# Up-projections with high and low activations in one stream of 512 columns, and their two halves added on the way out

## The chip, the cores and the metric

The kernel runs on one core of a Trainium2 chip. The metric is the device time of one launch in microseconds, the median of several runs. The core has a matrix engine (TensorE, PE in the profile; its weight loads are listed as PEld), a vector engine (VectorE, DVE), a scalar engine (ScalarE, ACT), GpSimd (POOL) and SyncE (SP), which mostly issues DMAs. In the trace each engine runs its instructions in program order, and engines wait for each other through semaphores.

## What is computed

The reference is banded attention (each row sees itself and the 63 rows before it), then a dense two-layer network with ELU, then a mixture of eight experts in which each token goes to one.

```python
x = attention(q, k, v)                       # 4 batches x 576 rows, 8 heads of 64 -> (2304, 512)
h = x @ w_in                                 # (2304, 2048)
g = np.where(h > 0, h, np.exp(np.minimum(h, 0)) - 1)
x = g @ w_out                                # (2304, 512)
logits = x @ w_gate + modality_bias[modality_id]
e_idx = argmax(logits); gate_w = softmax(logits)[e_idx]
for e in range(8):
    out[e_idx == e] = gate_w * (np.maximum(x[e_idx == e] @ w1[e], 0) @ w2[e])
```

## The kernel before

Every product of the two networks is made of three: an operand `a` is split into a high part and a low part (`hi` and `a - hi`), and the kernel adds high x high, high x low and low x high. The dense network runs over nine groups of 256 tokens and eight pieces of 256 hidden columns, 72 pairs of an up piece and a down piece. The experts run over slots: eight slots of 256 tokens with four up and four down pieces each, and a ninth, wide slot of 384 tokens.

An **up piece** (`h_pass`, called by `f1p` for the dense network and by `e1p` for the slots) makes 256 hidden columns for 256 tokens. For each half `c` of 128 hidden columns and each of the four blocks `d` of the model dimension it issues three matmuls of 256 columns: high weights on high x (L526), high weights on low x (L527), low weights on high x (L528). That is 24 matmuls into one PSUM bank of the pool `ps_h`, which has two. Each matmul has its own weight load. A **down piece** (`y_pass`, L535 to L537) is 12 matmuls of 512 columns into two banks `y`.

Between an up piece and its down piece of the dense network stand, in this order: `f1x` (the negative part of `h`, on ACT at L556 or on DVE at L558), `f1e` (exponential, ACT, L562), `f1m` (DVE, L571, from `e` and `h`), `f1h` (high part into `g`, ACT, L575) and `f1l` (low part, on POOL at L582 or on DVE at L580). The bank `h` is free again after `f1m`, except for the pieces listed in `VIA`, which keep their values in the bank up to `f1l`. In a slot it is shorter: `e1a` (Relu into the high part, ACT, L947), then `e1d` (low part, DVE, L952), and then the down piece `e2p`.

The order of the work on each engine isn't written by hand. `program` lists pieces with an engine, a cost, what they depend on, a rank and the buffers they take and free; `plan` goes through them in planned time, and on each engine starts the ready piece of lowest rank whose buffers are free. The code is then issued in that order. The buffer `L` is no memory: it keeps certain DVE and POOL pieces apart in the plan, but not on the chip. Everything but `sw` is known when the plan is made.

`switch` (piece `sw`) stands three times in each slot from slot 2 on. It reads a register that says whether the next slot has another expert, and only then splits new weights: for each of its tiles 128x1024 a copy on ACT (`e_hi`, L864) and a subtraction on DVE (`e_lo`, L868), two tiles in its first and last place, four in the middle one. Its cost in the plan is 0.3 us whether or not it is taken. With these inputs it is taken once, from slot 4 to slot 5.

The routing of the whole batch (`route_d` and `route2_d`, L759 to L841, small vectors on one partition) runs on DVE as two pieces, `rd` and `r2`.

Of the kernel before, what the change touches and what calls it, by code (L numbers as in the profile page):

```python
# [81 lines left out]
def fused(ctx, tc, q, k, v, w_in, w_out, mod, w_gate, mbias, w1, w2, out):  # L82
# [60 lines left out]
    gp = mkpool("g", 3)  # L143
# [289 lines left out]
    def x_at(t, qds):  # L433
        return (a[:, 2 * qds[0]:2 * qds[-1] + 2, 128 * (t % 2):128 * (t % 2) + 128] for a in X[t // 2])
# [13 lines left out]
    def new_x(g):  # L448
        X[g] = tuple(xp.tile([128, 4, 256], F32R, tag=n, name=n) for n in ("xh", "xl"))
# [62 lines left out]
    G, H, EL = {}, {}, {}  # L512
# [3 lines left out]
    def on_act(g):  # L516
        return g in FXA
# [241 lines left out]
    def route_d():  # L759
# [35 lines left out]
        RT["no"], RT["base"] = no, base  # L795

    def route2_d():
# [103 lines left out]
    def xpa(s, t):  # L901
# [124 lines left out]
    def program():  # L1026
# [79 lines left out]
        for g in range(NG):  # L1106
            for s in range(NP):
# [5 lines left out]
                add(("f1",) + k, "PE", 2.89, f1p, *k, rank=r + 1.5,  # L1113
                    deps=[("wd", "i", s, 0), ("wd", "i", s, 1)] + [("4d", 4 * g + x) for x in ((1, 3) if 2 * g >= T0 else range(4))] + ([("f1", g, s - 1)] if s else [("f1", g - 1 - (g < NG - 1), NP - 1)] if g > 1 else []),
                    need={"h": 1}, free=({"X": 1} if s == NP - 1 else {}) | ({"w": 2} if g == NG - 1 else {}), lat=0.22)
                add(("fx",) + k, "ACT" if on_act(g) else "DVE", 0.48 if on_act(g) else 0.6, f1x, *k, rank=r - 900, deps=[("f1",) + k], need={"e": 1})
# [39 lines left out]
        add("iota", "POOL", 0.6, iotas, rank=-700.0, deps=[("g3s", EC - 4)], need={"w": 1}, lat=0.5)  # L1156
        add("ep", "PE", 0.1, early_p, rank=-2000.0, deps=[("g3d", EC - 1)], need={"ps": 1}, lat=0.22)
# [109 lines left out]
```

## Time and profile before

| | |
|---|---|
| median of 3 runs | 738.29 us (738.16 to 739.16) |
| profiled execution, its own time | 738.16 us |
| its span, first to last instruction | 736.4 us |
| PE busy | 722.5 us, 98% |
| DVE busy | 429.7 us, 58% |
| ACT busy | 326.1 us, 44% |
| POOL busy | 192.7 us, 26% |
| mean granted TensorE clock | 0.998 |

The profiled execution is one launch; 1.8 us of its time lie outside the span. A busy engine has instructions under way, which tells nothing of how close they lie: the profile gives each matmul a modelled end and the ends overlap the next start, so for PE the distance from one start to the next is the number to read.

### The profile page before, as it was taken

The page shows a single profiled execution, that of the slowest core. Times are in us where ns is not written, and L with a number is a line of the kernel's source. Part 1 is how long each engine was busy: PE and PEld are TensorE (multiplying, and loading weights), DVE is VectorE, ACT ScalarE, POOL GpSimd, SP SyncE. Part 2 cuts the span into 40 slices and gives each one's busy share as a digit, 9 for nine tenths or more (in the row PEclk, how much of TensorE's full clock was granted, in tenths as well). Part 3 has the DMA queues.
Part 4 walks back from the last instruction along what each step waited for, and adds up shares of the span by engine and source line. Part 5 has one row for each costly group of instructions (what it writes and reads, how often), then busy time and mean ns, then how long its engine had stood idle before and what let it go on. Part 6 is the DMA issues. An engine that isn't in the chain of part 4 may idle for free. (4 is left out here: it accounts for less than half of the span.)

```text
span 736.4 us, 14731 instructions
## 1 busy us (share of the span) xinstructions
PE 722.5 (98%) x5550; PEld 649.7 (88%) x5550; DVE 429.7 (58%) x1324; ACT 326.1 (44%) x774; POOL 192.7 (26%) x184
## 2 busy tenths in 40 slices
PE   8899999999999999999999999999999999999996
PEld 7788988999899998989898998989988999999995
DVE  5999998688595194296394293793872124321211
ACT  5998753656565364454454433454111114311211
POOL 5211002334334233224233323431031212111011
PEclk9999999999999999999999999999999999999999
DMA  7999811632321131140210000550028112000001
GB/s 197 225 259 319 271 64 53 198 99 59 73 72 30 26 96 24 30 109 8 59 45 1 12 18 6 194 140 20 15 69 305 58 30 75 17 30 30 1 28 46
DMA packets 103102, 62.81 MB, mean 85 GB/s; under 512 B 85777, under 2 KB 90019, under 8 KB 102891
## 3 DMA queue, kind: packets, MB, share of 16 engines
q1 hardware_dynamic: 99403, 52.03, 26.1%
q0 software_dynamic: 3616, 9.72, 4.0%
q8 instruction: 46, 0.75, 0.4%
q14 instruction: 37, 0.30, 0.1%
HBM read 51.05 MB, written 10.94 MB: 84 GB/s over the span
## 5 line engine op out<-in xcount | busy, mean ns | idle before, releaser
L526 PE MATMUL h<-xh,whi 128*128 128x256 f32 x576 | 165.6, 287 | 0.4 <-DVE g L580 0.4
L528 PE MATMUL h<-xh,wlo 128*128 128x256 f32 x576 | 162.9, 283 | 0.0
L527 PE MATMUL h<-xl,whi 128*128 128x256 f32 x576 | 162.9, 283 | 0.0
L582 POOL TENSOR_TENSOR g<-e,g 128x512 fp32r<-128x512 f32 x57 | 80.0, 1403 | 190.8 <-ACT g L575 167.1
L535 PE MATMUL y<-whi,g 128*128 128x512 f32 x288 | 116.0, 403 | 0.0
L536 PE MATMUL y<-wlo,g 128*128 128x512 f32 x288 | 112.7, 391 | 0.0
L537 PE MATMUL y<-whi,g 128*128 128x512 f32 x288 | 112.5, 391 | 0.0
L526 PEld LDWEIGHTS h<-xh,whi 128*128 128x128 f32 x576 | 110.1, 191 | 2.4 <-PE h L528 0.6
L527 PEld LDWEIGHTS h<-xl,whi 128*128 128x128 f32 x576 | 110.3, 191 | 1.3
L528 PEld LDWEIGHTS h<-xh,wlo 128*128 128x128 f32 x576 | 110.2, 191 | 0.1
L571 DVE SCALAR_TENSOR_TENSOR e<-e,h 128x512 f32<-128x512 f32 x57 | 39.1, 686 | 85.6 <-ACT e L562 72.0
L612 DVE CUSTOM_DVE_ANT_0 lgs<-ysb,wgb 128x512 bf16<-128x512 f32 x96 | 79.5, 828 | 2.5 <-ACT ysb L599 0.6
L556 ACT ACTIVATE e<-h 128x512 f32<-128x512 f32 x64 | 38.1, 595 | 94.0 <-PE h L528 93.6
L952 DVE SCALAR_TENSOR_TENSOR g<-h,g 128x512 fp32r<-128x512 f32 x32 | 22.1, 690 | 86.6 <-ACT g L947 86.5
L526 PE MATMUL h<-xh,ehi 128*128 128x256 f32 x256 | 72.6, 284 | 0.0
L528 PE MATMUL h<-xh,elo 128*128 128x256 f32 x256 | 72.4, 283 | 0.0
L527 PE MATMUL h<-xl,ehi 128*128 128x256 f32 x256 | 72.4, 283 | 0.0
L947 ACT ACTIVATE g<-h 128x512 fp32r<-128x512 f32 x32 | 19.1, 597 | 112.8 <-PE h L528 104.2
L537 PEld LDWEIGHTS y<-whi,g 128*128 128x128 f32 x288 | 54.1, 188 | 12.1
L535 PEld LDWEIGHTS y<-whi,g 128*128 128x128 f32 x288 | 54.2, 188 | 10.8 <-issue 1.5
L390 ACT ACTIVATE sm<-sm,st 128x128 f32<-128x128 f32 x144 | 56.0, 392 | 17.4 <-DVE st L383 17.4
L536 PEld LDWEIGHTS y<-wlo,g 128*128 128x128 f32 x288 | 54.3, 189 | 9.0
(216 smaller groups left out, 1393.3 us busy)
## 6 DMA issues: line engine op xcount, KB each, us to landing
raw<-in_moe_w_in_dram SPq DMA_DIRECT2D x16, 512.0 KB, 5.4
raw<-in_moe_w_out_dram SPq DMA_DIRECT2D x16, 512.0 KB, 5.6
wraw<-in_moe_w_dram SPq DMA_DIRECT2D x16, 512.0 KB, 5.6
v<-in_v_dram SPq DMA_DIRECT2D x46, 128.0 KB, 2.7
kq<-in_k_dram SPq DMA_DIRECT2D x30, 128.0 KB, 2.8
kq<-in_q_dram SPq DMA_DIRECT2D x30, 128.0 KB, 3.2
yd<-ysb SPq DMA_DIRECT2D x12, 256.0 KB, 2.8
v<-in_v_dram SPq DMA_DIRECT2D x44, 64.0 KB, 3.5
```

Source lines behind the costliest of these rows:

```text
L390: act(out=sm[:, h], in_=sm[:, h], func=AF.Exp, bias=st[:, 0, h:h + 1], scale=-1.0, accum_out=st[:, 1, h:h + 1])
L526: mm(hs[c], w[0][:, d, f], xh, start=d == 0, stop=False)
L527: mm(hs[c], w[0][:, d, f], xl, start=False, stop=False)
L528: mm(hs[c], w[1][:, d, f], xh, start=False, stop=d == 3)
L535: mm(y, gh[:, m], w[0][:, c], start=first and c == 0, stop=False)
L536: mm(y, gh[:, m], w[1][:, c], start=False, stop=False)
L537: mm(y, gl[:, m], w[0][:, c], start=False, stop=last and c == 1)
L556: act(out=e, in_=H[g, s], func=AF.Relu, scale=-1.0)
L571: dve.scalar_tensor_tensor(out=h if via_psum(g, s) else e, in0=e, scalar=-1.0, in1=h, op0=ALU.add, op1=ALU.max)
L582: pool.tensor_tensor(out=a[:, 1], in0=e, in1=a[:, 0], op=ALU.subtract)
L612: dve.tensor_tensor_reduce(out=lgs, in0=y, in1=wgb[:, e], scale=1.0, scalar=0.0, op0=ALU.mult, op1=ALU.add, accum_out=GT[t][:, e:e + 1])
L952: dve.scalar_tensor_tensor(out=g[1][:, c], in0=h, scalar=0.0, in1=g[0][:, c], op0=ALU.max, op1=ALU.subtract)
```

## The change

The high and low x of a group now lie side by side in one tile `x` of [128, 4, 2, 256] in place of the two tiles `xh` and `xl`. For the dense groups 2 to 8 (`SPG`) and for slots 0 to 7, an up piece becomes two half pieces, `f0`/`f1` and `e0`/`e1`, one for each 128 hidden columns (`h_split`). A half has four matmuls of 512 columns (high weights on high and low x) and four of 256 (low weights on high x). It fills one bank: the products with high x in its first 256 columns, those with low x in its second 256. ACT copies the second to an SBUF tile `hs` (`h_out`), and DVE adds the first to it (`h_sum`), which frees the bank. `f1x`, `f1m`, `e1a` and `e1d` then read `hs` instead of the bank. Groups 0 and 1 and the wide slot keep `h_pass`.

The up pieces of the groups and slots no longer wait for one another in the plan's dependences, but for the down piece four pieces back (`AHD`). The pool `g` has two buffers instead of three, and `hs` two. The low parts made from the bank (`VIA`) are the first nine pieces instead of fifteen, `f1x` of group 5 moves from DVE to ACT, and several ranks and two ranges of the weight conversion differ. The routing is handed to the plan in five pieces instead of two.

```diff
-    EXR = -622.1
-    XDR = -853.02
+    EXR = -514.55
+    XDR = -825.93
-    SG = 20.7
+    SG = 22.67
-    UR = (0.86, 0.83)
-    HE = range(24, 32)
-    LE = range(0, 27)
-    VIA = range(0, 15)
+    UR = (1.04, 0.87)
+    HE = range(26, 32)
+    LE = range(0, 28)
+    SPG = range(2, 9)
+    AHD = 4
+    VIA = range(0, 9)
...
-    FXA = (0, 1, 2, 3, 4, 6, 7, 8)
+    FXA = (0, 1, 2, 3, 4, 5, 6, 7, 8)
...
-    gp = mkpool("g", 3)
+    gp = mkpool("g", 2)
+    hsp = mkpool("hs", 2)
...
-        X[g] = tuple(xp.tile([128, 4, 256], F32R, tag=n, name=n) for n in ("xh", "xl"))
+        X[g] = x_tile()
+
+    def x_tile():
+        return xp.tile([128, 4, 2, 256], F32R, tag="x", name="x")
...
+    def h_split(x, w, c):
+        h = h_tile()
+        f = slice(128 * c, 128 * c + 128)
+        for d in range(4):
+            mm(h, w[0][:, d, f], x[:, d], start=d == 0, stop=False)
+            mm(h[:, 0], w[1][:, d, f], x[:, d, 0], start=False, stop=d == 3)
+        return h
+
+    def h_sum(key, c):
+        h = HC.pop(key + (c,))
+        dve.tensor_tensor(out=H[key][:, c], in0=h[:, 0], in1=H[key][:, c], op=ALU.add)
+
+    def h_out(key, c):
+        if c == 0:
+            H[key] = hsp.tile([128, 2, 256], F32, tag="hs", name="hs")
+        act(out=H[key][:, c], in_=HC[key + (c,)][:, 1], func=AF.Copy)
+
+    def f0p(g, s, c):
+        HC[g, s, c] = h_split(X[g], WI[s], c)
...
+    def e0p(s, j, c):
+        HC["e", s, j, c] = h_split(XE[s], we(j), c)
...
-        return g * NP + s in VIA
+        return g * NP + s in VIA and g not in SPG
...
+                    deps.append(("f2",) + divmod(i - AHD, NP))
+                    add(("f0",) + k, "PE", 1.385, f0p, *k, 0, rank=r + 1.45, deps=deps, need={"h": 1}, lat=0.22)
+                    add(("f1",) + k, "PE", 1.385, f0p, *k, 1, rank=r + 1.5, deps=deps, need={"h": 1}, free=done, lat=0.22)
+                    for c in range(2):
+                        add(("fc",) + k + (c,), "ACT", 0.3, f0a, *k, c, rank=r - 900, deps=[("f1",) + k, ("fc",) + k + (0,)] if c else [("f0",) + k],
+                            need={} if c else {"hs": 1})
+                        add(("fa",) + k + (c,), "DVE", 0.34, f0d, *k, c, rank=r - 900, deps=[("fc",) + k + (c,)] + ([("fa",) + k + (0,)] if c else []),
+                            free={"h": 1})
...
+                    add(("e0", s, j), "PE", 1.385, e0p, s, j, 0, rank=500.0 + k + j + 1.45, deps=deps, need={"h": 1}, lat=0.22)
+                    add(("e1", s, j), "PE", 1.385, e0p, s, j, 1, rank=500.0 + k + j + 1.5, deps=deps, need={"h": 1},
+                        free=done, lat=0.22)
...
-        add("rd", "DVE", 4.5, route_d, rank=RDR, deps=["rp"], need={"w": 1}, lat=0.5)
-        add("r2", "DVE", 6.3, route2_d, rank=R2R, deps=["rd"], need={"w": 1}, free={"ps": 1}, lat=0.5)
+        part = {"rd": route_d(), "r2": route2_d()}
+        for n, x, c in (("rd", 0, 2.0), ("rd", 1, 2.5), ("r2", 0, 2.1), ("r2", 1, 2.1), ("r2", 2, 2.1)):
+            add((n, x), "DVE", c, next, part[n], rank=RDR if n == "rd" else R2R, deps=[(n, x - 1) if x else ("rp",) if n == "rd" else ("rd", 1)],
+                need={} if x else {"w": 1}, free={"ps": 1} if n == "r2" and x == 2 else {}, lat=0.5)
```

Two places show how the order moves. In the rows below, a name without number is a tile, `x2` is a count, and the rows from TENSOR_LOAD to the second branch are `switch`.

ACT in slot 4, around the middle `switch`, which splits the tiles of slot 5. Before: the copies of the gathered x (L912), the Relu of up piece 2 (L947), the switch, and the Relu of up piece 3 and of slot 5's piece 0.

```order
L947 ACTIVATE g<-h 128x512
L912 ACTIVATE xh<-p_x 128x4x128 x2
L947 ACTIVATE g<-h 128x512
L874 TENSOR_LOAD arena
L874 ISA x2
L984 COMPARE_AND_BRANCH
L864 ACTIVATE ehi<-wraw 128x1024 x4
L984 UNCONDITIONAL_BRANCH x2
L947 ACTIVATE g<-h 128x512 x2
```

After: L575 is `h_out` of one half, L996 the Relu from `hs`, L902 `e_hi`.

```order
L575 ACTIVATE hs<-h 128x256 x2
L996 ACTIVATE g<-hs 128x512
L575 ACTIVATE hs<-h 128x256
L912 TENSOR_LOAD arena
L912 ISA x2
L1033 COMPARE_AND_BRANCH
L902 ACTIVATE ehi<-wraw 128x1024 x4
L1033 UNCONDITIONAL_BRANCH x2
L575 ACTIVATE hs<-h 128x256
```

The switch stood between the Relus of pieces 2 and 3; now it stands between the copies of the two halves of piece 3, and the Relu of piece 3 comes after the second copy.

DVE at the same place, before: L952 is `e1d`, L868 `e_lo`.

```order
L952 SCALAR_TENSOR_TENSOR g<-h,g 128x512
L922 TENSOR_TENSOR xl<-p_x,xh 128x4x128 x2
L952 SCALAR_TENSOR_TENSOR g<-h,g 128x512
L874 TENSOR_LOAD arena
L984 COMPARE_AND_BRANCH
L868 TENSOR_TENSOR elo<-wraw,ehi 128x1024 x4
L984 UNCONDITIONAL_BRANCH x2
L952 SCALAR_TENSOR_TENSOR g<-h,g 128x512 x2
```

After: L570 is `h_sum`, L1001 is `e1d` from `hs`, L906 `e_lo`.

```order
L570 TENSOR_TENSOR hs<-h,hs 128x256 x2
L1001 SCALAR_TENSOR_TENSOR g<-hs,g 128x512
L570 TENSOR_TENSOR hs<-h,hs 128x256
L912 TENSOR_LOAD arena
L1033 COMPARE_AND_BRANCH
L906 TENSOR_TENSOR elo<-wraw,ehi 128x1024 x4
L1033 UNCONDITIONAL_BRANCH x2
L570 TENSOR_TENSOR hs<-h,hs 128x256
L1001 SCALAR_TENSOR_TENSOR g<-hs,g 128x512
```

Before, `e1d` of piece 3 follows the four subtractions of the switch; now the sum of piece 3's second half stands between them.

DVE in the dense network, at the first tile's rank (`g3d`: L654 before, L687 after). Before: L395 and L396 belong to attention, L612 to the gate's logits.

```order
L612 ISA lgs,lr<-ysb,wgb 128x512
L612 ISA lr 128x1
L395 TENSOR_SCALAR st<-st 128x4
L396 RECIPROCAL st<-st 128x4
L654 TENSOR_TENSOR r<-p_rk,ebase 128x8
L655 ISA r,f<-r,oh 128x8
L655 ISA f 128x1
L657 CAST fi<-f 128x1
```

After: L604 is `f1m`, L570 `h_sum`, L667 and L668 the gate's weight.

```order
L604 SCALAR_TENSOR_TENSOR e<-e,hs 128x512
L570 TENSOR_TENSOR hs<-h,hs 128x256
L687 TENSOR_TENSOR r<-p_rk,ebase 128x8
L688 ISA r,f<-r,oh 128x8
L688 ISA f 128x1
L690 CAST fi<-f 128x1
L667 TENSOR_SCALAR sc<-sc 128x1
L668 RECIPROCAL ent<-sc 128x1
L398 TENSOR_SCALAR st<-st 128x4
L399 RECIPROCAL st<-st 128x4
L570 TENSOR_TENSOR hs<-h,hs 128x256
```

`f1m` now reads `hs`, and between two sums `h_sum`, each of which frees a bank, stand `g3d` and small work of the gate and of attention.

## Rows read from the trace of the kernel before

**Rows 1.** The page, part 1: busy us (share of the span) and instructions of each engine.

```profile
PE 722.5 (98%) x5550; PEld 649.7 (88%) x5550; DVE 429.7 (58%) x1324; ACT 326.1 (44%) x774; POOL 192.7 (26%) x184
```

**Rows 2.** Who PE waited for: engine, line, releaser: total us, times, longest.

```profile
PE p_a L409 <- POOL sm L401: 1.7, 2, 1.0
...
PE p_s L372 <- DVE kq L351: 0.2, 1, 0.2
```

**Rows 3.** Groups by line: operands, form, count, busy us, mean ns, idle before.

```profile
L526 PE MATMUL h<-xh,whi 128*128 128x256 f32 x576 | 165.6, 287 | 0.4 <-DVE g L580 0.4
...
L526 PE MATMUL h<-xh,ehi 128*128 128x256 f32 x256 | 72.6, 284 | 0.0
```

**Rows 4.** Timeline, 301 to 309 us, PE and POOL: start, us, instruction, idle before.

```profile
301.75 0.28 PE L526 MATMUL h<-xh,whi 128*128 128x256 f32 x1
...
304.62 0.40 PE L535 MATMUL y<-whi,g 128*128 128x512 f32 x1
...
306.92 0.39 PE L536 MATMUL y<-wlo,g 128*128 128x512 f32 x1
...
307.37 1.03 PE L345 MATMUL p_t<-ident,kq 128*128 128x128 f32 x8
...
307.67 1.29 POOL L582 TENSOR_TENSOR g<-e,g 128x512 fp32r<-128x512 f32 x1 [4.32 <-ACT g L575]
...
308.16 0.36 PE L526 MATMUL h<-xh,whi 128*128 128x256 f32 x1
...
308.37 0.28 PE L527 MATMUL h<-xl,whi 128*128 128x256 f32 x1
```

**Rows 5.** Groups by line and form: ACT and DVE, instructions like the added ones.

```profile
L908 ACT ACTIVATE xwh<-p_x 128x256 fp32r<-128x256 f32 x6 | 1.8, 400 | 2.6 <-PE p_x L899 2.6
...
L919 DVE TENSOR_TENSOR xwl<-p_x,xwh 128x256 fp32r<-128x256 f32 x6 | 2.1, 414 | 2.6 <-ACT xwh L908 2.6
...
L947 ACT ACTIVATE g<-h 128x512 fp32r<-128x512 f32 x32 | 19.1, 597 | 112.8 <-PE h L528 104.2 <-PE y L537 5.0 <-PE p_rk L642 3.5
...
L952 DVE SCALAR_TENSOR_TENSOR g<-h,g 128x512 fp32r<-128x512 f32 x32 | 22.1, 690 | 86.6 <-ACT g L947 86.5
...
L612 DVE CUSTOM_DVE_ANT_0 lgs<-ysb,wgb 128x512 bf16<-128x512 f32 x96 | 79.5, 828 | 2.5 <-ACT ysb L599 0.6
```

**Rows 6.** Timeline, 602 to 626 us, ACT, DVE and PE: slot 4 and the change of expert.

```profile
602.08 0.40 PE L535 MATMUL y<-ehi,g 128*128 128x512 f32 x1
...
602.27 0.60 ACT L947 ACTIVATE g<-h 128x512 fp32r<-128x512 f32 x1 [5.02 <-PE h L528]
...
617.13 0.60 ACT L947 ACTIVATE g<-h 128x512 fp32r<-128x512 f32 x1 [4.96 <-PE h L528]
617.87 1.06 ACT L864 ACTIVATE ehi<-wraw 128x1024 fp32r<-128x1024 f32 x1
619.89 2.96 ACT L864 ACTIVATE ehi<-wraw 128x1024 fp32r<-128x1024 f32 x3 [0.95 <-PE h L527]
...
619.81 0.40 PE L535 MATMUL y<-ehi,g 128*128 128x512 f32 x1
...
620.98 3.50 DVE L868 TENSOR_TENSOR elo<-wraw,ehi 128x1024 fp32r<-128x1024 f32 x3 [0.79 <-ACT ehi L864]
624.40 0.68 DVE L952 SCALAR_TENSOR_TENSOR g<-h,g 128x512 fp32r<-128x512 f32 x1
...
625.43 0.40 PE L535 MATMUL y<-ehi,g 128*128 128x512 f32 x1
```

**Rows 7.** Two DVE lines: count, duration ns min/median/max, first and last start.

```profile
L612 DVE CUSTOM_DVE_ANT_0 lgs<-ysb,wgb x96: 658/691/2327, 140.0 to 530.8; 128x512 bf16<-128x512 f32 x96
...
L571 DVE SCALAR_TENSOR_TENSOR e<-e,h x57: 654/687/690, 136.5 to 504.1; 128x512 f32<-128x512 f32 x57
```

**Rows 8.** Stretches: length, busy us of PE, PEld, DVE, ACT, POOL, PEclk, DMA.

```profile
150.00:200.00 50.00, 50.00 (x461) 44.42 (x458) 37.53 (x167) 30.20 (x91) 21.07 (x17) 1.00 0.28 62
730.00:737.00 7.00, 0.00 (x0) 0.00 (x0) 0.00 (x0) 0.00 (x0) 0.97 (x1) 0.76 0.21 75
```

More of the change, by code (lines that the diff above doesn't have):

```diff
@@ L433, in x_at @@
     def x_at(t, qds):
-        return (a[:, 2 * qds[0]:2 * qds[-1] + 2, 128 * (t % 2):128 * (t % 2) + 128] for a in X[t // 2])
+        return (X[t // 2][:, 2 * qds[0]:2 * qds[-1] + 2, z, 128 * (t % 2):128 * (t % 2) + 128] for z in range(2))
     def a4a(t, qds, eng):
@@ L795, in route_d @@
         RT["no"], RT["base"] = no, base
+        yield
     def route2_d():
@@ L910, in xpa @@
         if t == 0:
-            XE[s] = [xp.tile([128, 4, 256], F32R, tag=n, name=n) for n in ("xh", "xl")]
-        act(out=XE[s][0][:, :, m], in_=p, func=AF.Copy)
+            XE[s] = x_tile()
+        act(out=XE[s][:, :, 0, m], in_=p, func=AF.Copy)
     def xpd(s, t):
@@ L926, in exs, with e0a, e0d @@
             return lambda d: tuple(a[:, d % 2] for a in XE[s][d // 2])
-        return lambda d: tuple(a[:, d] for a in XE[s])
+        return lambda d: (XE[s][:, d, 0], XE[s][:, d, 1])
+    def e0p(s, j, c):
+        HC["e", s, j, c] = h_split(XE[s], we(j), c)
+    def e0a(s, j, c):
+        h_out(("e", s, j), c)
+    def e0d(s, j, c):
+        h_sum(("e", s, j), c)
+        if c:
+            H[s, j] = [(H.pop(("e", s, j)), slice(0, 2))]
     def e1p(s, j):
@@ L1112, in program @@
                 via = via_psum(g, s)
[L1113 to L1116, printed above, removed]
+                deps = ([("wd", "i", s, 0), ("wd", "i", s, 1)] + [("4d", 4 * g + x) for x in ((1, 3) if 2 * g >= T0 else range(4))]
+                        + ([("f1", g, s - 1)] if s and g not in SPG else [("f1", g - 1 - (g < NG - 1), NP - 1)] if g > 1 else []))
@@ L1117, in program @@
+                add(("fx",) + k, "ACT" if on_act(g) else "DVE", (0.52 if split else 0.48) if on_act(g) else 0.6, f1x, *k, rank=r - 900,
+                    deps=[("fa",) + k + (1,) if split else ("f1",) + k], need={"e": 1})
                 add(("fe",) + k, "ACT", 0.52, f1e, *k, rank=r - 900, deps=[("fx",) + k])
-                add(("fm",) + k, "DVE", 0.6, f1m, *k, rank=r - 900, deps=[("fe",) + k], free={"e": 1} if via else {"h": 1})
-                add(("fh",) + k, "ACT", 0.5 if via else 0.52, f1h, *k, rank=r - 900, deps=[("fm",) + k], need={"g": 1})
+                add(("fm",) + k, "DVE", 0.6, f1m, *k, rank=r - 900, deps=[("fe",) + k],
+                    need=L if split else {}, free={"e": 1} if via else L | {"hs": 1} if split else {"h": 1})
@@ L1120, in program @@
+                add(("fh",) + k, "ACT", 0.5 if via else 0.52, f1h, *k, rank=r - 900,
+                    deps=[("fm",) + k] + ([("fh",) + divmod(i - 1, NP)] if split else []), need={"g": 1})
                 if via:
@@ L1208, in program @@
                 add(("pf", s), "SP", 0.5, prefetch, s, rank=k - 900,
[L1209 to L1210 removed]
+                    deps=[("r2", 2)] + ([("ex", j) for j in range(8)] + [("xa", EA)] if s == EA - 1 else [("sw", s, 2)]))
+        caps = {"w": 33, "ps": 4, "h": 2, "y": 1, "P": 2, "v": 3, "ld": 2, "PA": 2, "X": 3, "e": 2, "g": 2, "hs": 2,
                 "gs": 3, "ix": 5, "L": 1}
```

61 lines of the change are left out of this document (40 added, 21 removed).

## Prediction

> **What bounds the kernel now.** I read the page's first part, then PE's waits, then the distance between matmul starts in the timeline, and last the queues of ACT and DVE where PE depends on them. PE is under way in 98% of the span [rows 1]. Nine releasers account for all its visible waits, the first for 1.7 us and the last for 0.2 us [rows 2], together 6.4 us, nearly all of it in the first 100 us. From there on PE runs matmul after matmul, so what a PE instruction costs goes into the time at full price, and what ACT, DVE or POOL do costs nothing until PE waits for it. DVE, the busiest of the others, has 37.5 of 50 us at 150 to 200 us [rows 8].
>
> **Up pieces.** The pace is read from starts. An up piece of 24 matmuls of 256 columns runs from 301.75 to 304.62, 2.87 us or 119.6 ns each; a down piece of 12 matmuls of 512 columns runs from 304.62 to 307.37, 2.75 us or 229 ns each, and its last two take 225 ns each [rows 4]. Two matmuls of 256 columns thus take 239 ns and one of 512 takes 225 to 229 ns: a pair saves 10 to 14 ns. L526 ran 576 times in the dense network, of which seven of nine groups change, 448, and 256 times in the eight slots, which all change [rows 3]: 704 pairs, 8 in each of 88 up pieces. The gain is 7.0 to 9.9 us; I take 12 ns, **-8.4 us**. The 256-column matmul of low weights that now stands between two of 512 keeps its 119.6 ns.
>
> A rule of the Trainium skill speaks against so much. Its page "TensorE: Matmul & The Clock Gate", section "Back-to-back issue gap", gives the gap between two matmul starts at full clock as the columns at 2.4 GHz plus 2.5 ns, so a merged pair would save only those 2.5 ns, an estimate of 1.8 us for 704 pairs, and the sum below would end 6.6 us higher. The trace disagrees with it on both forms, 119.6 and 229 ns where the rule has 109 and 216, and the measurement decides.
>
> **More changes between small and large work on PE.** After eight transposes the first large matmul holds PE for 0.21 us (308.16 to 308.37) where the pace is 0.12 [rows 4]. In PE's order such a change comes 82 times after and 75 times before, since halves give more places to put small work. 7 x 0.09 us: **+0.6 us**.
>
> **What replaces the read of the bank.** Each half adds a copy on ACT (128x256 from PSUM, 400 ns) and an addition on DVE (128x256, one operand in PSUM, 414 ns) [rows 5], 176 of each, so 70 and 73 us of engine time. ACT and DVE have 410 and 307 us of the span left [rows 1], so this costs nothing but where PE waits for it. There are three such places.
>
> First the bank. With two banks, a half may start when the bank of the half before last is free. The copy starts about 0.19 us after the half's end (PE begins the next piece at 602.08, ACT the Relu at 602.27 [rows 6]), 0.40 and 0.03 to DVE, 0.41, about 0.1 back to PE: 1.13 us. The half that lies between takes 4 x 229 + 4 x 119.6 ns = 1.39 us. So three halves in a row, which come 35 times in PE's order with nothing of weight between them, fit with 0.26 us to spare if ACT and DVE are free, and not if a 0.6 us instruction stands in front.
>
> Second the chain to the down piece. In a slot it is 0.19 + 0.40 + 0.03 + 0.41 + 0.03 + 0.60 (Relu, L947) + 0.03 + 0.69 (L952) + 0.1 = 2.5 us [rows 5]; the shortest cover in PE's order is two halves, 2.78 us, in 12 of 32 cases. In the dense network the old chain ran from 304.62 to the end of POOL's subtraction, 307.67 + 1.29, so 4.3 us [rows 4]; with copy and sum it is 5.2. The shortest cover there is 5.5 us, and most are above 6.9. Both fit if nothing else is queued.
>
> What is queued comes third. `f1m` had one operand in the bank and now has both in SBUF. L612, with both in SBUF, has a median of 691 ns, a mean of 828 and a longest of 2327 [rows 5, 7]; L571 with `h` in PSUM never took over 690 [rows 7]. The mean excess is 0.137 us, the largest 1.64 us; 56 runs of `f1m` at that mean excess are 7.7 us more on DVE, behind which the next `h_sum` stands. Most of it falls into the slack above; if all reached PE it would be 7.7 us, if none, 0. I take **+1.0 us**, near the lower end because before the change PE's visible waits after the first 100 us came to about 1 us, with L612's long runs on the same queue.
>
> The Trainium skill, "SBUF — State Buffer", section "Who interferes with whom", says that a DVE instruction with two SBUF inputs and a GpSimd instruction that reads SBUF exclude each other for the whole instruction, and that one SBUF input is free of this. The two lines agree with it. By it, a collision can cost up to POOL's whole 1.29 us, not the mean.
>
> **The change of expert.** Here the sum has its second large term. In slot 4 the middle switch is taken. Before: ACT copies one tile at 617.87 ahead of the end of up piece 3 and three from 619.89 (2.96 us); DVE subtracts three from 620.98 to 624.48, then makes piece 3's low part, 624.40 to 625.08; PE, which ended the up piece at 619.81, starts the down piece at 625.43 [rows 6]. It had two pieces, 5.6 us, of cover, and 0.3 us of that were left.
>
> After, with T the end of up piece 3: ACT makes piece 2's Relu behind its second copy, up to T - 1.1, then the copy of piece 3's first half, and 0.74 us after that one's start (as from 617.13 to 617.87) the first of four weight copies, T - 0.4. At a step of 0.95 us they end at T + 3.5. DVE's four subtractions step by 1.14 us from T + 0.7 and end at T + 5.4. Only then come the sum of the second half (5.8), the Relu (6.4), the low part (7.1) and the down piece at T + 7.2. PE's cover is now one down piece and one half, 2.75 + 1.39 = 4.1 us. It waits 3.0 us. The first switch (two tiles) by the same steps: the down piece can start at 4.9, cover 2.75 + 0.86 (the transposes of the next slot) = 3.6, so 1.3 us. The last one (one tile free early, one late, with a 0.75 us output behind it): 0.7 us. Together **+5.0 us**, once. Bounds: 0 if ACT and DVE get through before PE needs them, 7.2 if each tile of the eight costs its full 0.9 us or so. I take the steps as they are, since they are those of this very place.
>
> **The rest at nothing.** Routing in five pieces moves the same 10.4 us of DVE work. `f1x` of group 5 moves 8 instructions of about 0.6 us to ACT, which has room. Fewer low parts from the bank take 6 x 0.7 us off DVE in the first 130 us, where PE is covered by other work. If that cover is gone, it is part of the 1.0 us.
>
> **The sum.** 738.16 - 8.4 + 0.6 + 1.0 + 5.0 = 736.4 us for the profiled execution (span 736.4, outside 1.8), which is 0.13 under the median of 738.29. I predict **736.4 us**, 0.26% less. About 0.2%, 1.5 us, is what a measurement can tell from no change, so the line is at 736.8.
>
> **Rivals.**
> A: the switches hide. If the copies and sums get past the splits, or the stall is a third of my figure, 5.0 becomes 0 to 1.7: 731.4 to 733.1 us. For it: before, the same splits fitted. Against: the order puts the sum behind them. Chance 0.27.
> B, slower: the bank, not the pace, decides. If `f1m` is stretched as L612 is, the next sum frees its bank late. From the point where a stretch exceeds the 0.26 us of slack at a row of halves, PE waits. With 4 to 7.7 us reaching PE: 739.4 to 743.1 us, slower. For it: DVE's 37.5 of 50 us at 150 to 200 [rows 8] grows by about 6. Against: halves rarely stand in a row there. Chance 0.20.
> C: the pair saves nothing, because one stream of 512 holds PE as long as two of 256: the gain of 8.4 is gone, 744.8 us. Against: 229 against 239 ns in this trace. Chance 0.05. By the page on TensorE named above the time would be 743.0 instead.
> D: the granted clock falls in the 3 us wait. It is 1.00 in all stretches with work and 0.76 in the last 7 us, when PE has stopped [rows 8]. At 1.2 instead of 2.4 GHz the next down piece takes 2.75 us more: 739.1 us. The same page of the skill, "What's actually happening", says that an idle engine goes to half clock; no run here shows it for a wait of this length. Chance 0.08.
> Forecast: 0.40, 734.5 to 738.5 us.
>
> **Numbers.** Faster: A 0.27 and two thirds of the forecast 0.26, 0.53. Same: forecast 0.14, B 0.05, D 0.06, 0.25. Slower: B 0.15, C 0.05, D 0.02, 0.22. The range reaches from the upper part of A to the middle of B: 731.0 to 742.0.
>
> **What would show it.** The pace: up pieces of halves at 2.78 us from start to start. The switch: a wait of about 3 us on PE before a down piece in slot 4, released by DVE's low part, with two smaller ones on either side; without it A holds. The bank: waits of L564 released by L570, and L604 with a longest duration far above 690 ns. Wrong would be a pace of 240 ns for a 512 and its share, or any new wait in the first 100 us, which I have not costed.

## The result and the profile after

| | before | after |
|---|---|---|
| median | 738.72 us (738.16 to 739.84) | 746.81 us (744.91 to 747.75) |
| profiled execution, its span | 736.4 us | 746.0 us |
| ratio to before, 95% interval | | 1.0104 (1.0077 to 1.0131) |

The changed kernel is slower by 1.0%. I had predicted 736.4 us with a range up to 742.0, so both the sign and the range were wrong. Page, part 1, after, beside [rows 1]:

```profile
PE 720.3 (97%) x4834; PEld 611.8 (82%) x4834; DVE 490.0 (66%) x1485; ACT 391.4 (52%) x960; POOL 211.1 (28%) x189
```

PE's waits after, in us, times and longest; [rows 2] had 6.4 us in ten waits, here it is 18.2 us in 24:

```profile
PE h L564 <- DVE hs L570: 3.7, 6, 1.6
PE y L542 <- ACT g L996: 2.8, 2, 2.4
PE p_rk L673 <- DVE sc L658: 2.6, 4, 1.6
```

Two of these releasers are new: the sum L570, which frees a bank, and the Relu L996 of the slots. The third is the gate's rank `p_rk`, whose matmul needs a chain of small gate instructions on DVE; it cost 0.6 us before. Where they lie is read from stretches. The rows give the length, then the busy us of PE, PEld, DVE, ACT and POOL, and the granted clock ahead of the last two columns. First before, then after:

```profile
0.00:100.00 100.00, 94.33 (x901) 81.98 (x902) 89.33 (x258) 77.41 (x205) 20.46 (x38) 1.00 0.88 244
...
400.00:500.00 100.00, 99.39 (x648) 90.16 (x647) 62.29 (x169) 43.56 (x73) 34.49 (x27) 1.00 0.25 69
...
600.00:700.00 100.00, 100.00 (x643) 91.47 (x642) 30.39 (x42) 26.94 (x43) 11.52 (x11) 1.00 0.09 28
```

```profile
0.00:100.00 100.00, 91.50 (x882) 79.41 (x883) 88.13 (x252) 76.91 (x204) 28.43 (x41) 1.00 0.85 236
...
400.00:500.00 100.00, 95.03 (x482) 78.71 (x481) 70.47 (x192) 51.91 (x103) 34.79 (x28) 1.00 0.21 69
...
600.00:700.00 100.00, 96.58 (x492) 80.86 (x492) 42.62 (x74) 37.33 (x74) 10.81 (x11) 0.98 0.08 28
```

PE's idle time, the length less its busy time, went from 5.7 to 8.5 us in the first 100 us, from 0.4 to 1.4 up to 250, from 0.6 to 5.0 between 400 and 500, and from 0 to 3.4 between 600 and 700. From 250 to 400 and from 500 to 600 it is 0 in both. Together that is 11.6 us more.

**The pace** is better than before, but less so than forecast. Timeline of PE, after, one up piece in two halves, from its first matmul to the transposes behind it:

```profile
301.79 0.39 PE L564 MATMUL h<-x,whi 128*128 128x512 f32 x1
302.01 0.28 PE L565 MATMUL h<-x,wlo 128*128 128x256 f32 x1
302.13 0.40 PE L564 MATMUL h<-x,whi 128*128 128x512 f32 x1
...
304.60 1.04 PE L348 MATMUL p_t<-ident,kq 128*128 128x128 f32 x8
```

The piece takes 2.81 us (301.79 to 304.60), where [rows 4] had 2.87. A 512-column step takes 0.23 us or a little more and the 256-column step behind it 0.12. 0.06 us in each of 88 pieces, taken from this one piece, is an estimate of 5.3 us gained, not 8.4.

**A late bank.** Timeline after, 483 to 490 us, the longest of the waits for L570:

```profile
484.74 2.46 DVE L906 TENSOR_TENSOR elo<-wraw,ehi 128x1024 fp32r<-128x1024 f32 x1
...
484.80 1.31 POOL L615 TENSOR_TENSOR g<-e,g 128x512 fp32r<-128x512 f32 x1
...
486.35 0.38 ACT L575 ACTIVATE hs<-h 128x256 f32<-128x256 f32 x1
...
487.12 0.68 DVE L645 CUSTOM_DVE_ANT_0 lgs<-x,wgb 128x512 bf16<-128x512 f32 x1
...
487.44 0.28 PE L565 MATMUL h<-x,wlo 128*128 128x256 f32 x1
...
487.73 1.21 DVE L906 TENSOR_TENSOR elo<-wraw,ehi 128x1024 fp32r<-128x1024 f32 x1
...
488.87 0.74 DVE L570 TENSOR_TENSOR hs<-h,hs 128x256 f32<-128x256 f32 x2
...
489.34 0.50 PE L564 MATMUL h<-x,whi 128*128 128x512 f32 x1 [1.62 <-DVE hs L570]
```

ACT has copied the first half out by 486.73. Its sum is next on DVE only at 488.87, because a low part of expert weights (`e_lo`, L906), a gate product (L645) and another low part stand ahead of it. L906 usually takes 1.22 us; the first one here takes 2.46, over the whole run of POOL's subtraction that began 0.06 us after it. PE has issued the other half by 487.44, both banks are full, and the next half begins at 489.34.

Not all of the 5.0 us at 400 to 500 are such waits: 2.5 us are released by the sum, and 2.4 us are waits of `p_rk` for the gate's chain in the same queue (0.6 us before). The longest of these, timeline after:

```profile
496.99 1.23 DVE L652 CUSTOM_DVE_ANT_0 lg<-lr,bias 128x8 f32<-128x8 f32 x1
...
499.01 0.17 PE L673 MATMUL p_rk<-oh,tri 128*128 128x8 bf16 x1 [1.59 <-DVE sc L658]
```

L652, the first of the gate's chain, usually takes 0.17 us; beside POOL's L615 it took 1.23 here. A sum stood behind that chain too and ended at 499.35, so the bank would not have come sooner.

**The change of expert.** Timeline after, 624 to 636 us, slot 4:

```profile
624.89 3.90 ACT L902 ACTIVATE ehi<-wraw 128x1024 fp32r<-128x1024 f32 x4 [0.66 <-issue]
...
625.98 4.63 DVE L906 TENSOR_TENSOR elo<-wraw,ehi 128x1024 fp32r<-128x1024 f32 x4 [1.05 <-ACT ehi L902]
...
627.74 0.39 PE L564 MATMUL h<-x,ehi 128*128 128x512 f32 x1
...
629.03 0.28 PE L565 MATMUL h<-x,elo 128*128 128x256 f32 x1
630.53 0.42 DVE L570 TENSOR_TENSOR hs<-h,hs 128x256 f32<-128x256 f32 x1
630.98 0.63 ACT L996 ACTIVATE g<-hs 128x512 fp32r<-128x512 f32 x1 [1.92 <-DVE hs L570]
...
631.67 0.79 PE L542 MATMUL y<-ehi,g 128*128 128x512 f32 x1 [2.36 <-ACT g L996]
...
632.26 0.63 PE L543 MATMUL y<-elo,g 128*128 128x512 f32 x1
...
632.68 0.63 PE L544 MATMUL y<-ehi,g 128*128 128x512 f32 x1
...
635.96 0.39 PE L564 MATMUL h<-x,ehi 128*128 128x512 f32 x1
```

It is the chain of the prediction: four copies (L902), four subtractions (L906), then the sum that stands behind them (630.53), its Relu (630.98), and then the down piece at 631.67, released by the Relu. PE had one down piece and one half to cover this, and waited 2.36 us. The matmuls behind the wait start 0.42 us apart, not 0.23. The granted clock:

```profile
630.00:632.00 2.00, 0.33 (x1) 0.34 (x2) 1.30 (x3) 1.02 (x3) 0.00 (x0) 0.84 0.00 0
632.00:634.00 2.00, 2.00 (x6) 1.47 (x6) 1.77 (x3) 0.87 (x1) 0.00 (x0) 0.50 0.00 0
634.00:636.00 2.00, 2.00 (x9) 1.60 (x8) 0.12 (x1) 0.00 (x0) 0.00 (x0) 0.81 0.00 0
```

The down piece takes 4.29 us (631.67 to 635.96), 2.75 in [rows 4]: the lower of the two clock levels, 0.50, cost 1.5 us here.

**The sum.** 5.3 us gained by pace, 11.6 us more idle time, 1.5 us by the clock: +7.8 of the span's +9.6 us. The rest would fit the starts behind waits: the first matmul after a wait holds PE longer (0.50 us at 489.34, where its like take 0.40), and there are 14 more waits; at an estimated 0.1 us each that is 1.4 us.

### The profile page after: what moved, and what is told of

The parts are those of the page before. It is cut to its first block, busy times and chain, and to the rows that moved or that the text cites. A ratio compares the mean times of both kernels' runs of the same rounds, so it can differ in the third digit from the quotient of the medians.

```text
span 746.0 us, 13704 instructions
## 1 busy us (share of the span) xinstructions
PE 720.3 (97%) x4834; PEld 611.8 (82%) x4834; DVE 490.0 (66%) x1485; ACT 391.4 (52%) x960; POOL 211.1 (28%) x189
## 5 line engine op out<-in xcount | busy, mean ns | idle before, releaser
L564 PE MATMUL h<-x,whi 128*128 128x512 f32 x448 | 164.4, 405 | 3.1 <-DVE hs L570 3.1
L615 POOL TENSOR_TENSOR g<-e,g 128x512 fp32r<-128x512 f32 x63 | 98.7, 1566 | 221.6 <-ACT g L608 210.7
L570 DVE TENSOR_TENSOR hs<-h,hs 128x256 f32<-128x256 f32 x176 | 73.9, 421 | 109.7 <-ACT hs L575 107.9
L575 ACT ACTIVATE hs<-h 128x256 f32<-128x256 f32 x176 | 66.9, 380 | 140.3 <-PE h L565 130.5
L565 PE MATMUL h<-x,wlo 128*128 128x256 f32 x448 | 125.4, 280 | 0.0
L564 PEld LDWEIGHTS h<-x,whi 128*128 128x128 f32 x448 | 84.2, 188 | 23.5 <-DVE hs L570 4.8
L564 PE MATMUL h<-x,ehi 128*128 128x512 f32 x256 | 91.9, 399 | 0.6 <-DVE hs L570 0.6
L565 PEld LDWEIGHTS h<-x,wlo 128*128 128x128 f32 x448 | 84.6, 189 | 1.2
L645 DVE CUSTOM_DVE_ANT_0 lgs<-ysb,wgb 128x512 bf16<-128x512 f32 x96 | 74.4, 775 | 1.1
L565 PE MATMUL h<-x,elo 128*128 128x256 f32 x256 | 71.8, 280 | 0.0
L393 ACT ACTIVATE sm<-sm,st 128x128 f32<-128x128 f32 x144 | 56.0, 391 | 18.2 <-DVE st L386 17.5
L564 PEld LDWEIGHTS h<-x,ehi 128*128 128x128 f32 x256 | 48.1, 188 | 12.3 <-DVE hs L570 0.9
L542 PE MATMUL y<-ehi,g 128*128 128x512 f32 x128 | 51.6, 403 | 2.8 <-ACT g L996 2.8
```

The costliest lines, as they stand in the source:

```text
L393: act(out=sm[:, h], in_=sm[:, h], func=AF.Exp, bias=st[:, 0, h:h + 1], scale=-1.0, accum_out=st[:, 1, h:h + 1])
L542: mm(y, gh[:, m], w[0][:, c], start=first and c == 0, stop=False)
L564: mm(h, w[0][:, d, f], x[:, d], start=d == 0, stop=False)
L565: mm(h[:, 0], w[1][:, d, f], x[:, d, 0], start=False, stop=d == 3)
L570: dve.tensor_tensor(out=H[key][:, c], in0=h[:, 0], in1=H[key][:, c], op=ALU.add)
L575: act(out=H[key][:, c], in_=HC[key + (c,)][:, 1], func=AF.Copy)
```

## The experiments

The theory after this reading: the change loses in three separate places, the bank and the gate's rank behind DVE's queue at 428 to 500 us (5 us), the taken switch (5 us with the clock), and the first 100 us (2 to 3 us), and gains 5 us by pace. The rival: DVE and POOL have too much to do whatever the banks are, or the changed order of the plan is at fault and not the halves. The table gathers what all runs gave, under short names; idle us of PE is the length of a stretch less PE's busy time, read as above. Each run has its order planned anew, so other work moves a little with every edit.

| run | ratio to before (95%) | 0 to 100 | 100 to 250 | 250 to 400 | 400 to 500 | 500 to 600 | 600 to 700 |
|---|---|---|---|---|---|---|---|
| before | 1 | 5.7 | 0.4 | 0 | 0.6 | 0 | 0 |
| after | 1.0104 (1.0077 to 1.0131) | 8.5 | 1.4 | 0 | 5.0 | 0 | 3.4 |
| x1 switch behind | 1.0058 (1.0036 to 1.0081) | 7.0 | 1.4 | 0 | 4.9 | 0 | 0.3 |
| x2 slots whole | 1.0066 (1.0045 to 1.0086) | 7.6 | 1.4 | 0 | 5.2 | 0 | 0 |
| x3 dense whole | 1.0078 (1.0060 to 1.0096) | 7.5 | 1.1 | 0 | 1.1 | 0 | 3.1 |
| x4 512s first | 1.0125 (1.0108 to 1.0142) | 7.2 | 1.4 | 0 | 5.4 | 0 | 3.5 |
| x5 groups 7, 8 whole | 1.0057 (1.0036 to 1.0078) | 7.1 | 1.4 | 0 | 1.0 | 0 | 3.0 |
| x6 = x1 + x5 | 0.9991 (0.9981 to 1.0001) | 6.3 | 1.4 | 0 | 1.1 | 0 | 0.6 |
| x7 = x6, early constants of before | 1.0051 (1.0034 to 1.0067) | 5.7 | 0.4 | 4.7 | 0.5 | 0 | 0.3 |
| x7b = x6, conversion constants of before | 1.0084 (1.0069 to 1.0099) | 5.7 | 2.6 | 4.2 | 0.5 | 0 | 0.3 |
| x9 no halves | 1.0026 (1.0013 to 1.0039) | 7.6 | 1.1 | 0 | 1.1 | 0 | 0 |
| x10 = x6 + x4 | 0.9982 (0.9971 to 0.9992) | 8.7 | 1.4 | 0 | 1.0 | 0 | 0.6 |
| x11 = x7b + x4 | 1.0062 (1.0048 to 1.0076) | 5.8 | 2.6 | 4.4 | 0.5 | 0 | 0.3 |
| x12 routing in two | 1.0208 (1.0193 to 1.0223) | 7.3 | 1.4 | 0 | 5.0 | 4.5 | 3.5 |

### One place at a time: x1, x2, x3, x5

x1 gives each switch more to wait for, so that it is planned behind the low parts of the pieces before it:

```diff
-                    dp = [[("e1", s - 1, 1), ("pf", s - 1)], [("e1", s - 1, 3), ("e2", s - 1, 1), ("sw", s, 0)],
-                          [("e2", s - 1, 3), ("sw", s, 1)]][x]
+                    dp = [[("e1", s - 1, 1), ("eb", s - 1, 1), ("pf", s - 1)],
+                          [("e1", s - 1, 3), ("e2", s - 1, 1), ("eb", s - 1, 3), ("sw", s, 0)],
+                          [("e2", s - 1, 3), ("eb", s, 0), ("sw", s, 1)]][x]
```

> The branch code of a switched slot is placed behind the DVE and ACT work of the slot ahead (its low parts), so nothing of that work stands behind the taken branch. Theory, that the bank queue and the switch together made the loss: the waits of 0.50, 2.52 and 0.76 us between 615 and 640 us (3.8 us) shrink to under 1 us, the granted clock does not fall to 0.50 behind them (1.6 us of slow down-pieces), and the time falls by 4 to 5 us, to 742 to 743 us. Rival, that the switch waits only stand in for something else that is late (a transfer, the slot's own up pieces): the waits move, and the time stays within 1 us of 746.8.

Measured 742.16 us beside 737.77 of before, 0.46% less than the changed kernel against its own before, some 3.4 us. The theory's step holds; its size, 4 to 5 us, was a little high. Idle time at 600 to 700 us falls from 3.4 to 0.3 us and the clock stays at 1.00. PE's wait for the Relu of a slot:

```profile
PE h L564 <- DVE hs L570: 3.1, 5, 1.6
...
PE y L542 <- ACT g L996: 0.3, 1, 0.3
```

The waits for the bank in the dense part are untouched (3.1 us; the changed kernel's sixth wait, 0.6 us, lay in the slots). So the switch is one loss by itself.

x2 runs the slots with `e1p` as before, x3 the dense groups with `f1p`, x5 only groups 7 and 8:

```diff
...
-                if wide:
-                    add(("e1", s, j), "PE", 4.2, e1p, s, j, rank=500.0 + k + j + 1.5, deps=deps, need=hb, free=done, lat=0.22)
+                if True:
+                    add(("e1", s, j), "PE", 4.2 if wide else 2.89, e1p, s, j, rank=500.0 + k + j + 1.5, deps=deps, need=hb, free=done, lat=0.22)
...
-                add(("ea", s, j), "ACT", 0.52 * f, e1a, s, j, rank=k + j - 900, deps=[("e1", s, j) if wide else ("ew", s, j, 1)],
+                add(("ea", s, j), "ACT", 0.52 * f, e1a, s, j, rank=k + j - 900, deps=[("e1", s, j)],
...
```

```diff
-    SPG = range(2, 9)
+    SPG = range(9, 9)
```

```diff
-    SPG = range(2, 9)
+    SPG = range(2, 7)
```

> The expert slots run their up pieces in one piece of three 256-column matmuls per weight pair, as before; the dense groups 2 to 8 keep the split. Theory: the 5.4 us at the switch (3.8 us of waits, 1.6 us of halved clock) go, and the early slots' bank waits too (about 2 us), against 32 pieces that lose 0.063 us each (2.0 us): 741 to 743 us. Rival, that the loss lies in the pace of the split pieces or in the dense part alone: 747 to 749 us, the 2.0 us of pace lost with nothing back.

> The dense groups 2 to 8 run whole, as before, and only the expert slots are split. Theory: the waits for a bank between 428 and 500 us (6.0 us, 0.8 us before) fall back under 2 us and those between 100 and 420 us to 0.6 us, 5 to 5.5 us back, against 56 pieces that lose 0.063 us each (3.5 us): 744 to 746 us, with the waits at the switch as they were. Rival, that the dense stalls come from the changed constants and order of other work and not from the halves: the stalls stay and the time rises to 749 to 750 us.

> Groups 7 and 8 alone run whole (16 pieces), groups 2 to 6 and the slots stay split. Theory, that a half's bank is freed only after a sum that queues on DVE behind gate, low-part and routing work: the waits of 6.0 us between 428 and 500 us fall under 2 us, at a loss of 16 times 0.063 us (1.0 us): 742 to 744 us. Rival, that DVE and POOL are merely too full in that stretch whatever the bank does: the waits stay, now before down pieces and gates, and the time is 747 to 748 us.

Measured 742.55, 743.36 and 741.72 us beside the same 737.77. In all three the expected column of the table changes and the others stay, but for the first, which lies between 7.1 and 8.5 us from run to run. With whole slots no wait is left at the switch; the 2 us of bank waits that I expected in the early slots were not there to be saved (idle 0 at 500 to 600 us in both). With groups 7 and 8 whole, idle time at 400 to 500 us falls from 5.0 to 1.0 us, all of it now waits of `p_rk`; with all dense groups whole it falls to 1.1. The gates, low parts and POOL's work of that stretch are still there, and PE hardly waits for them. That speaks against both forms of the rival. What it doesn't separate is the two things that the halves of a piece bring: the shorter cover of a bank, and two sums more on DVE (70 us of work in those 100 us with halves, 64 without).

### What the constants cost and buy: x9, x6, x7, x7b

x9 joins the edits of x2 and x3, so no piece is split, while constants, buffers and routing stay as changed.

> No piece is split: all up pieces run as before, under the constants, the buffers (two gate tiles, two of the new sums, unused) and the five routing pieces of the change. Theory: what is left is the first 100 us, 2.5 to 3.5 us over before, 740 to 741.5 us, with PE steps of 120 ns throughout and no wait at the switch. Rival, that constants and routing pieces cost nothing by themselves: 738 us, the time of before.

Measured 740.30 us beside 737.94, 0.26% more (0.13 to 0.39). The first 100 us hold 7.6 us of idle time, 5.7 before. So about 2 us of the loss have nothing to do with the halves. (The 8.5 us of the changed kernel hold 2.2 us of waits for DMAs, where before has 1.0; this part differs from one execution to the next.) Of PE's waits, these two do not stand in [rows 2]:

```profile
PE p_t L348 <- ACT PA L352: 1.5, 1, 1.5
...
PE y L544 <- DVE g L613: 1.0, 1, 1.0
```

x6 joins x1 and x5.

> Both edits at once: the branch code stands behind the low parts, and groups 7 and 8 run whole. Theory, that the bank waits of 428 to 500 us and the switch are two separate losses: the gains of 3.3 and 3.7 us add, 738 to 739 us. Rival, that both hand time to the same later wait: one of the gains is lost, 741 to 742 us.

Measured 737.19 us beside 737.94, ratio 0.9991 (0.9981 to 1.0001). The two gains add: 0.0046 and 0.0047 alone, 0.0113 together, more than their sum by less than the intervals allow to tell. The loss of the change is gone, and it took only these two places.

x7 sets six constants of x6 back:

```diff
-    SG = 22.67
+    SG = 20.7
...
-    UR = (1.04, 0.87)
-    HE = range(26, 32)
-    LE = range(0, 28)
+    UR = (0.86, 0.83)
+    HE = range(24, 32)
+    LE = range(0, 27)
...
-    VIA = range(0, 9)
+    VIA = range(0, 15)
...
-    LG = 10.95
+    LG = 11.18
```

> As the run with both edits, and the constants UR, HE, LE, VIA, SG and LG stand as in the kernel before, which makes DVE's and ACT's order of the first 100 us equal to that of before. Theory, that the 3 us more of waits in the first 100 us come of those constants and not of the halves: the waits of 1.5, 1.1 and 0.5 us at 48, 96 and 44 us go, 735 to 736.5 us, faster than before. Rival, that the earlier order of the constants was what made room for the halves: as much is lost between 100 and 250 us, and the time stays at 738 to 739 us or above.

Measured 741.59 us: the rival was right. The first 100 us come back to 5.7 us of idle time, as before the change, but 4.7 us open up between 250 and 400, of which 2.9 are released by sums and 1.8 by the gate's chain. Timeline of x7, one of these waits:

```profile
274.30 1.74 POOL L615 TENSOR_TENSOR g<-e,g 128x512 fp32r<-128x512 f32 x1 [3.28 <-ACT g L608]
...
274.94 1.65 DVE L645 CUSTOM_DVE_ANT_0 lgs<-ysb,wgb 128x512 bf16<-128x512 f32 x1
...
276.63 1.40 DVE L645 CUSTOM_DVE_ANT_0 lgs<-ysb,wgb 128x512 bf16<-128x512 f32 x1
276.72 0.38 ACT L575 ACTIVATE hs<-h 128x256 f32<-128x256 f32 x1 [0.82 <-PE h L565]
...
278.69 0.42 DVE L570 TENSOR_TENSOR hs<-h,hs 128x256 f32<-128x256 f32 x1
...
279.17 0.49 PE L564 MATMUL h<-x,whi 128*128 128x512 f32 x1 [1.07 <-DVE hs L570]
```

The half is copied by 277.10, and its sum comes at 278.69, behind gate products (L645) that take 1.65 and 1.40 us beside POOL instead of 0.69. It is the same late bank, at another place. So the constants of the change cut both ways: they lose 2 us at the start and keep the halves of the dense part clear of the gate.

x7b sets back only UR, HE, LE and VIA, and leaves SG and LG as changed.

> The switch behind the low parts, groups 7 and 8 whole, and the four constants of the weight conversion (UR, HE, LE, VIA) of before; the gate's two (SG, LG) stay as changed. Theory, that SG and LG place the gate's logits away from the halves, and that moving them back made the bank waits of 0.7 to 1.2 us at 278, 287, 322, 338, 377 and 393 us: these go, and the first 100 us keep the 2 us of before, 735 to 736 us. Rival, that it is the conversion constants which shift the whole dense part against the attention: the waits stay, 740 to 742 us.

Measured 744.47 us beside 738.11. The theory on SG and LG falls: the waits between 250 and 400 us stay (4.2 us, of which 2.7 are now for the gate's rank), and one of 2.0 us for a bank comes at 163, behind which the granted clock fell to 0.50. It is the constants of the weight conversion that decide how the dense part meets the gate. Which of the four was not tried.

### What a pair of widths costs: x4, x10, x11

x4 changes the order in a half:

```diff
         for d in range(4):
             mm(h, w[0][:, d, f], x[:, d], start=d == 0, stop=False)
+        for d in range(4):
             mm(h[:, 0], w[1][:, d, f], x[:, d, 0], start=False, stop=d == 3)
```

> Each half issues its four 512-column matmuls first and its four 256-column ones behind them, instead of one of each in turn; nothing else differs from the changed kernel. Theory, that the turn from one width to the other is what eats the forecast saving (the 512 step takes 235 ns here and 228 ns among its like): a half falls from 1.405 to about 1.39 us, 176 halves give 2.5 to 3 us, 742.5 to 743.5 us. Rival, that each step costs what it costs whatever stands next to it: a half stays at 1.40 us and the time at 745 to 747 us.

Measured 747.27 us beside 737.94, no gain. The pace itself did gain. Timeline of x4, one piece, from its first four 512s to the transposes behind it:

```profile
299.95 1.07 PE L564 MATMUL h<-x,whi 128*128 128x512 f32 x4
...
302.73 1.04 PE L348 MATMUL p_t<-ident,kq 128*128 128x128 f32 x8
```

299.95 to 302.73 is 2.78 us, where the turns take 2.81, so 0.03 us for each of 88 pieces or 2.6 us. Part of that was lost to a second fall of the clock, behind the wait for p_rk at 495 to 497 us, where it stayed at 1.00 in the changed kernel:

```profile
498.00:500.00 2.00, 2.00 (x7) 1.62 (x7) 1.77 (x10) 0.00 (x0) 0.17 (x1) 0.50 0.00 0
```

At the price of the switch, 1.5 us, a gain of 1 us should be left, and none is seen; the two intervals overlap, so this run alone doesn't settle the order's worth. x10 is x6 with this order, x11 is x7b with it.

> The switch behind the low parts, groups 7 and 8 whole, and each half issues its four 512-column matmuls first. In the run that changed the order alone a half's shortest time fell from 1.400 to 1.379 us, but the granted clock fell to 0.50 behind a wait of 1.8 us at 497 us and no time was gained. Theory, that the order is worth 3.4 ns a pair once no long wait hides it: 576 pairs, 2.0 us less than the run with the first two edits, 735 to 735.5 us, 0.3 to 0.4% faster than before. Rival, that the order is worth nothing: 737 us, ratio 0.999.

> The two runs named above in one: switch behind, groups 7 and 8 whole, 512-column matmuls first, and the conversion constants of before. If both theories hold, 733 to 734.5 us, 0.5 to 0.7% faster than before; if only the order holds, 738 to 740 us.

x10 measured 736.73 us beside 738.11, ratio 0.9982 (0.9971 to 0.9992). It has the lowest ratio of all, 0.2% below before and below the changed kernel by more than the intervals. Against x6 it is lower by 0.0009 (0.7 us), less than the 2.0 us I expected, and the two intervals overlap, so the order's worth stays unshown; its profile has 8.7 us of idle time in the first 100 us and x6's 6.3, which can hide a gain. x11 measured 742.69 us, above both of its forecasts: it has the waits of x7b and is lower by 0.0022, again with overlapping intervals.

### A long piece ahead of a sum: x12

```diff
-        part = {"rd": route_d(), "r2": route2_d()}
-        for n, x, c in (("rd", 0, 2.0), ("rd", 1, 2.5), ("r2", 0, 2.1), ("r2", 1, 2.1), ("r2", 2, 2.1)):
...
+        add(("rd", 1), "DVE", 4.5, lambda: list(route_d()), rank=RDR, deps=[("rp",)], need={"w": 1}, lat=0.5)
+        add(("r2", 2), "DVE", 6.3, lambda: list(route2_d()), rank=R2R, deps=[("rd", 1)], need={"w": 1}, free={"ps": 1}, lat=0.5)
```

> The changed kernel with its routing in two pieces again (4.5 and 6.3 us in the plan), nothing else. DVE then has both routing pieces in one row in slot 1, with two sums and two low parts behind them that stood between before. Theory, that a bank which waits for a sum turns every long DVE piece into a PE wait: 3 to 6 us of new waits near 505 to 520 us, 749 to 753 us. Rival, that slot 1 has enough pieces in hand: 746 to 747 us as the changed kernel.

Measured 753.05 us beside 738.11, 0.0104 or 7.7 us above the changed kernel, at the upper end of the theory. Timeline of x12: the copy of a half, its sum, and the half that needs the bank:

```profile
545.75 0.38 ACT L575 ACTIVATE hs<-h 128x256 f32<-128x256 f32 x1 [0.74 <-PE h L565]
...
549.74 0.73 DVE L570 TENSOR_TENSOR hs<-h,hs 128x256 f32<-128x256 f32 x2
...
550.20 0.50 PE L564 MATMUL h<-x,ehi 128*128 128x512 f32 x1 [4.49 <-DVE hs L570]
```

The copy ends at 546.13 and the sum starts at 549.74; between them DVE runs routing instructions of at most 0.29 us each. PE waits 4.49 us, and the granted clock fell behind that wait:

```profile
552.00:554.00 2.00, 2.00 (x8) 1.71 (x8) 0.70 (x2) 0.73 (x2) 1.62 (x2) 0.50 0.90 312
```

The two profiled spans differ by 4.1 us, the ratios by 7.7. So the five routing pieces, which I had put at nothing, are worth some 4 to 8 us to a kernel with halves; in the kernel before, the two long pieces cost PE nothing (idle 0 at 500 to 600 us).

## Why the prediction was wrong, step by step

**The pace, -8.4 us: right in kind, 3 us too much.** A pair saved 7.5 ns, not 12. I had taken 225 to 229 ns for a 512-column matmul from a down piece, where it stands among its like, and 119.6 ns for the 256-column one. In turns the two take 351 ns, not 347, and with the 512s first a piece takes the 2.78 us of the prediction (x4). The bound of 7.0 us was too narrow for the same reason: both its ends came from rows of unmixed widths. The rule of the Trainium skill, "TensorE: Matmul & The Clock Gate", section "Back-to-back issue gap", by which I had 1.8 us, does not hold here: 2.87 and 2.81 us a piece. I had also read it too widely, since the section gives it for an isolated matmul and says that a stream with a weight load for each matmul is spaced otherwise. Nor do the about 131 ns that it states there for 512 columns agree with the 225 to 229 of this trace.

**Changes between small and large work, +0.6 us:** not separable. The estimate of 1.4 us above is for the starts behind waits, a term that the prediction lacked.

**The bank, +1.0 us with bounds 0 to 7.7: the step that failed.** The chain from a half's end to its free bank was right, and so was the slack of 0.26 us for three halves in a row "if ACT and DVE are free, and not if a 0.6 us instruction stands in front". Then I asked only what `f1m` would do, and that was the wrong instruction: L604's longest of 56 was 1.17 us, its median 0.69. What stood in front were `e_lo`, gate products and small gate instructions, which the kernel before had in the same stretch. PE's waits after the first 100 us came to about 1 us there, and I carried that over as the price. But the cover itself was halved by the change: where a whole piece filled a bank in 2.87 us and gave it to `f1m`, a half fills one in 1.41 us and waits for a DVE instruction just the same. Measured in place of the 1.0 us are 5.3 us more idle time from 100 to 500 us. Of PE's waits there, 3.1 us are released by sums, and 2.6 us (0.6 before) are for the gate's rank, a releaser that the prediction did not name. x5 shows that the halves are the cause: with groups 7 and 8 whole it has 4 us less idle time. That it is their shorter cover more than their added sums is argued from the timeline and not shown. Rival B named the wait, a sum that frees its bank late, but laid it to a stretched `f1m`; its place, 150 to 200 us, was not where it hit, and its price, 4 to 7.7 us, was about right. It had 0.20.

**The change of expert, +5.0 us: right in kind, 1.6 us too much.** Forecast were waits of 1.3, 3.0 and 0.7 us; idle time at 600 to 700 us is 3.4 us, in waits of 0.46, 2.36 and 0.59. The first two were released one step earlier than I said, by the Relu and not by the low part. Without the 0.7 us of the low part my steps give 0.6 and 2.3. The third was for a bank (L570).

**Rival D came true.** The clock fell behind that wait, for 1.5 us where I had priced 2.75. I had given it 0.08 because no trace of before had such a wait, and I treated it as an alternative to the forecast; it is a consequence of the forecast's own wait and should have been added to it with its chance. The Trainium skill, "TensorE: Matmul & The Clock Gate", section "What's actually happening", says that an idle engine goes to half clock; the rows at 632 to 634 us agree for this wait.

**"Which I have not costed": the first 100 us.** Ten profiles with the changed constants have 6.3 to 8.7 us of idle time there, four with those of before 5.7 to 5.8. The difference, about 2 us, is x9's ratio too. I had the new constants in the diff and called them free.

**Routing in pieces, at nothing:** 4 to 8 us in favour of the change (x12), which I did not see because the kernel before had no wait there.

Put together by the measured terms, with the estimate of 1.4 us as the last: 736.4 - 5.3 + 0.95 (100 to 250 us) + 4.4 (400 to 500) + 3.4 (switch) + 1.5 (clock) + 2.8 (first 100 us of this execution) + 1.4 = 745.6 us, against a span of 746.0.

## What to carry to other kernels

When a change cuts a step of the bounding engine into smaller ones, the cover of everything that frees their buffers is cut with it: list every instruction that can stand ahead of the freeing one in its queue, not only those the change edits, and compare each with the new, shorter cover. A plan that counted costs for other pieces hides a branch, a stretch beside another engine or a long routine; place these behind the freeing instruction, or split them (x12), or leave the coarse form in the stretch where they crowd. In this kernel two such places took back more than the gain, and without them (x6, x10) the time is that of before or just below.

## What the runs showed that I had not expected

The clock doesn't always fall behind a wait of the same length. x3 and x5 both waited 2.07 us at the same down piece of slot 4. Timeline of x3, and its granted clock in the stretch behind the wait (1.00, the third number from the end):

```profile
627.75 0.50 PE L542 MATMUL y<-ehi,g 128*128 128x512 f32 x1 [2.07 <-ACT g L996]
```

```profile
628.00:630.00 2.00, 2.00 (x9) 1.31 (x9) 1.78 (x3) 0.94 (x1) 0.00 (x0) 1.00 0.00 0
```

The same of x5, whose clock fell in the stretches behind it:

```profile
625.15 0.50 PE L542 MATMUL y<-ehi,g 128*128 128x512 f32 x1 [2.07 <-ACT g L996]
```

```profile
626.00:628.00 2.00, 2.00 (x7) 1.56 (x8) 1.38 (x2) 0.34 (x1) 0.00 (x0) 0.66 0.02 4
628.00:630.00 2.00, 2.00 (x6) 1.62 (x5) 0.00 (x0) 0.08 (x1) 0.00 (x0) 0.50 0.00 0
```

What decides between them is open.

A DVE instruction with two inputs in SBUF ran two to three times its usual time beside POOL's L615: 2.46 us for L906 (median 1.22), 2.22 us for L645 (median 0.69), while the eleven L906 that no L615 overlapped took 1.21 to 1.23. That agrees with the Trainium skill, "SBUF — State Buffer", section "Who interferes with whom", as far as the two get in each other's way; that the one issued first blocks the other is not seen, since the L906 of 484.74 began 0.06 us ahead of L615 and was the one to run long. `f1m`, of which I had feared it, took at most 1.17 us:

```profile
L604 DVE SCALAR_TENSOR_TENSOR e<-e,hs x56: 680/692/1174, 149.7 to 510.4; 128x512 f32<-128x512 f32 x56
```

No run took POOL's work away, so how much of the late sums is this stretch and how much the queue alone wasn't measured.
